# Inverse spectra in DRAM kept by partition, all of step 4 stored, and a new order of the first loads

## The chip, the cores and the metric

One core of a Trainium2 chip runs the kernel. The metric is device time in microseconds: the median of 3 runs of the kernel before is 442.58 us (442.55 to 443.0). One further execution was profiled: it took 444.42 us, of which its span, from the first to the last instruction that the profiler saw, is 442.6 us. All times below that stand beside a place in the schedule are counted from the start of that span. Lines are those of the kernel before.

## What is computed

The kernel is the forward and backward pass of two branches on the same input, S = 2048 tokens, D = 512, F = 1376. All ten results are returned: the output and nine gradients.

```python
xn = layernorm(q)
# branch A: a long convolution over tokens and channels, by FFT
k_shift = sum_t pad(k)[t:t+S] * shift_k[:, 3-t]
kv = k_shift * v
y  = irfft2(rfft2(pad(kv)) * rfft2(pad(ssm_k)))[:S] + kv * ssm_D
A  = xn * y
# branch B: a bilinear GLU
h  = (xn @ w_gate) * (xn @ w_up)
B  = h @ w_down
out = q + A + B            # and jax.vjp of this for grad_out
```

## The kernel before

**Layout.** The 2048 tokens stand as 128 partitions by R = 16 rows. F is cut into 6 steps j of 256 columns (step 1 has 96), in the order of the list `SF`. Everything lives in one SBUF tile `big` (and one PSUM tile `PP`), so the profile names nearly every tile `big`, and nearly every instruction carries line 172, the recording helper. Tiles are told apart by the DRAM tensor at the other end of a transfer, by shape and by time.

**Stages.** (1) Head: `xload`, `gtload`, `gload` and the weights arrive; `ln` (L369) computes the row statistics and normalises x in place; `tr_rows` (L384) transposes two rows on TensorE; `mlp_rows` (L391) does the matmuls of a row pair with the weights of step j. (2) `glu_gen` goes through the 6 steps. The three products of a row (h, and two factors for the gradients) go into a ring of 24 slots in SBUF, `ring(j, r)` (L273), and `hd_store` (L408) writes them to the DRAM tensor HD, four rows at a time: one store of 768 KB. Steps 0, 2 and 3 and the narrow step 1 are stored whole; of step 4 (NST - 2) only the rows below `KEEP` = 8; step 5 is not stored. `dw_all(j)` computes the weight gradients of a step, 96 matmuls. (3) Branch A's transform in three DRAM passes: `a_gen` (first DFT, about 25 to 125 us, into AX), `s_gen` (about 130 to 275 us): it loads AX, does the middle DFT `s_B`, the products `s_pw`, the inverse middle DFT `s_Bi` with the table ET, and stores the inverse spectra to the DRAM tensor CX. (4) `turn_gen` (L559) transposes the products that were not stored on TensorE, 128 by 128 each, 8 to a PSUM tile, with one ACT copy for each 8: 8 rows of step 4 and 16 rows of step 5, 6 blocks a row, 144 transposes and 18 copies. (5) F, from about 290 us: 8 chunks n of two rows. `c_load(n)` (L613) brings 1536 KB of CX into `f["C"]`, `last_dft` (L652) does the last DFT with the table W2, and `c_y`, `c_dkv`, `c_o5`, `c_dsk`, `dk_pair` make branch A's outputs. `y_o` and `y_x` (L719, L732) do 33 matmuls of 128x512 a row with the transposed products.

**How HD comes back.** `hd_load(m)` (L581) is a transposing DMA of one row m: 640 columns for an even row and 512 for an odd one while m < KEEP, 512 and 384 from there on (the missing 128 columns are step 4's, turned on TensorE). Even rows have two buffers `hdE` (each also holds a part that the odd row beside it reads), odd rows have one buffer, `hdO`. So the load for row 2n + 3 can start only when row 2n + 1 has been multiplied.

**How CX lies.** CX has 128 by 32 entries of 3 KB (three signals of 512 columns), each padded to 3,136 bytes. The first index is a frequency q = 4g + k, the second a row index r of 32. `s_Bi` leaves a tile whose partition is (k, r); it is stored through the view `(g k) r e -> (k r) g e`: neighbouring partitions write neighbouring entries. A chunk's load reads, for each of 128 q, two pairs of entries, 100,352 bytes apart from one q to the next.

**What sets the order.** The program is first recorded as operations with a due time (`at(t)`), and `emit` then issues them in the order that the string `PLAN` holds (it also holds the PSUM place of each tile). All DMAs, loads, stores and transposing loads alike, are issued by SyncE (SP), in that order, so one that waits holds back all behind it. The first loads have due times from -10 on, in the order of L341 to L355. 32 matmuls on a tile of ones (8 of 512 columns, 24 of 128; L319 to L323) come ahead of any data.

Of the kernel before, what the change touches and what calls it, by code (L numbers as in the profile page):

```python
# [11 lines left out]
F32 = mybir.dt.float32  # L12
ALU = mybir.AluOpType
# [16 lines left out]
KEEP = 8  # L30
EPS = 1e-5
PLAN = "c-lpG0~98^?{<;~UE8*8+qP}nwr$(CZQHi(y?1y2@4NSRzHg?JO!M?fnw*|aCpI7e!~uf1kOtyGd`JKe5(0yOLLxBm5CTF%C<qN<AS{G~@DKqaLL`U`Q6MTrgXoYIVn9rY1*IV|WP|Kb268|W$O-wO9^`_gkOy)@eaH(1pfV(bd{7X|LKP?kRUtW)hr&<}ia<3e3dNv06o=-J0xCcWr~x&h7Sx7H&<RpPNoWDRpboTz&d>mQLtUr{sh}0~fkx088bTZB3*Dd{^n=DQ4oX26Xae0~0i=eu&=vYaQy2>EVIcH?W-tsoz`rm6IzmsF0pnpIM8cUc9MZ!em;fVT5sZL|Fc=oYBp3yoVF;v!$uJty!5CNtOCU4Mf+?^Xrovd51505xEQ94R4d%iYSOL>vD`bIruoAYxeAo+XAOmcNeXtI8z*^V^J7GV3hV}3fzQArc02$#RY=k|q0gl2~I0VPx8)SlGa2QU)5jX+g;WC_pi|`xH!Fjj>Kj0EvfYT5U<6{C$h-aV+cEv<^4IaQ%_z8(|6LiCe&>eeVXzYoP;2*dSk0A-3qojBPlHnit1<CO&5T?MCm<m%PVj4_~PvADB!(P}ML*P^BgLj}WJ_o>I_zXtiC+LU6u|JN)QP>zAHo?)@6dA|j7z~BYP;nDB#}?QUL*hefg@&!M4TizC*bdvHU<V9~v#}#~!Z{cYJx<5YI1|I;0GxpXaTX53!8i|ZLIfOwm9R3-#amDiBVuGMgoUvP-i4yL8dqQxya&bbK19XhSOQC8DU61tu?&{Qa#$XtV+E{&Rk0dY#8ns*W8fOBj&X1$*1(#00&8JyT#K==4mO~57#m-}D_D<p@g>y5xY&^D;|6Siuc0B<p+>k7H{%-^iU+YS)uVm*7T&`+d<XSu5`KUQI36csdYp(EFe6UIop=B<;S}73hwuw!#>F@dvtU*{j7u;Z?!oMs1CL-%%!Ru#H|D{km>2WmLfnh_@fdEwMOXj_(tO;8CvhoW!K-);uj388iMMbB-Nrk(AMfHlypIp?AwI&#_ynKgR(yuf@ddub<M;|+;~RX7@9;f-z}oZ?KjCNmf?x3)e#am96aT^O_%Hs#-}nau3xJ3mF$pOdc?v-xDHMgKFcg-;QFw|#3os%@qVu>6n@~Txh!-$2?Z8Xej0R8?DoLfNDV3%&G>FPlIch=8=`s$c<dlL^QYvamsVNPmr6H7#(o+V?NSP=zWudH;jmpzdsz4Q~5@n|xv>bC%E;@z7C^zMys5FoAQa;L01*jkuqLEaXiqLc_O2w!+Ri-LbmHJaPDnY}kI@O?P6rEyFO^QjeC^p5RMsynEQap-J3Fr(?p@fu(5>paNN@uY#b);l8o?6j4>_n}pElr|{)P~yA1nNoCr~|d58PuI7Q!naFqi81epf0qEu2C&oN3&=(eWl*ChQ`ut8bj-;E3KueG@9nn2AWUZXd~^Xy)=&I(gE5{eP|z@r=_%q4$>CtOBZMbEvId?j5g6B+D<F!B5kFgw3#l^zw{67qy==D&d@K~K}YEdEvB=yhz`>++C>ZLJ3XSSbexXR54uAy=>#pI-*l2<x>zo@yHAfPj*IK!xqB4f-K7NX8zpp!Tw?cxlDMQUnfpT_+*1nUPSFDj>DYyJ&jJfT+;eL0PE&H{+zU$KLb;Sq-E|7>I=Jxe26c3uTxWNay0}}^)eUsv+<UrBgIqWFkv>p&*TeO6y<BhiiTb#{uAdv~`n%8ciiWwtE|q&juPL=l<I=ixF1>q88C*t}$z^s!To(6^vbt<;xXbQxxSXz@tM78T2CkuN<Z`>lu8C{vnz`n#g=^_RTDjKl54Uk`U0GMowR7bixI8YeLzmCxcOzT@H_4fc;wC%q3c5%xs*B(vyD2W3i|AOUy6A4S6H$rb#=0@iWSkr6LWq}XZoC`iP^P;I&Iw6espu-Xcv9I_aaG+6SIt#-A*F_^>1w&!u8y1FX1Tg9tW0$CTxgl;R=7|y-z{+~-E6nag_osnj$7`+Nf?PQtK3|-*hP>+E};~5MO;KF>LN)omq3cU$dX7(xFk~2t#(^oR7orgTvFNQO1WfGLQ1>na@{R-#bu2v<D$q7mt1bTMedfn?bf<G?ykG%V#s~>z(tdXE~ccG0WOw2a%ttUd*WitQx`{`xik`*GfNmwC(m72&LZJBgM{Z}?zlVQ(o1%Uz$qk$oOD?wm7H>?T{b!6a>`kkQqH+da^B^VGLl;^xQtR(^2kMZ$>o*H?usiXS6z9@ClUFYi^LmTMS0;0N&#8tDo7#8FaNkA@~_+IN=ji_?|!*b(ou@ZZ}-O)l}-Y@$sv~(;?1sx)RV}(#nqB19F?Q7<GNB)n1w5eas#O%`(1r$B9&#YYb?eGTr;UE`<&;dQe8rDNNy+xT_Xv_&83cPch#hYymW_LH>oW<+$+~oUc2t{#<h~Su8q8N?_CdRE1l)A`{24td->=-xg+kg`{KIDSJzs;xpvZ1zPk?6TV~4-my72}FUiKaxxWmTpDsENkQf}3vvVwt!*O|_jFxyjLUM3y9wa$=jO=tnBoD{u!IFUcNM26JyWA*A#EE&N^phmK+a={>JXVr(UrE8kWUlOSDS5oilcO#ZkCUM?QRYiJ&cK;@f=rc3vRE>5Dqbq7ISZHIX);C9a4}BLOC&ANkWyTdC(A5ZAk(EZFO*}FmGkjYDZ_<$k<66*T!0JnMp-EZxj3(qqFjzwOA)TbTcrY*<;q;1*GNU)B-MDG)ZnVTR<=nkuEI6BIxmyj{EZv%7Fi*6xj!$L0lY&t$Ur_Wb+{q#l0m#)Hp^f>AwzhNwBnO8l()+;9?m1UH6M^uvQJv@PB|loWVeju(=v+B%4j|!E&08S;k`1J&&vlH$NQxox8Z{_o-fNesn6~Bu(an6d__9)9qGiKxeH&Fu6#jmOE<nG-MI%pke=L&@5@E$&G)1a_vO2CO&&=<KEgNTp&aE2e2kCt6FI@x<s?6rTk=Jo$tnIOr}?Iw;j{cy&hb}i#4qHdyp+cLouA8j{v>bY0$=1y{7NqKXKBXo<h6X4E8LW?adZADF*TOHm5JPzf5>mS&XX8)GMi4}2mD7+RUh(Hp2kk6b11#XA+-sU{v-E!2LF-}I+Jg)*D(5TU|X8Sp*6PN=Gh!hS?6$AjiYlpg3jalyny5C4GypIbRqxXoBW6)X?%^WcX%^L(=Ggy6X;e>s8KYAZsW&%UnA;v-oc4=Cr8y?yqov%6HcUiIlAuSB)Xq7Xfi#(2l)^$;-tEm(`zbS!iRY&XVPVSM^o!^&ZsLmo37+loJO~6R$a}>HHYrdyP93s@Ke60Yk3`~)DN6RGixqQq3b!FZs3i)S3mMyPOC3?6X(-?nnz#pRnDm|d8fYSPh3EEX<mKDx%CZy=KNY%|K<1mjEm|Q{>tUFh?du1Tuh&H1udw>b+^9didsnvX$h^YRkWj4)oQv&OKK-At(~=tcGYfLO1o<h?Ww)AtoGJE+E>eHKkcu-d4TTMfjUSB>jAB<HMFMI(%M=_>*^34s`Yf3F43jBOo!_TU9Ky1rLNMax?0!hT3x5>b%Soy-?~XR>uo)#TXeEc(L*{_r|ES4hiB+aou#vNj?UG2I$sy)LS3XIb(AjF(K<%Q>Np**^>u<y)CSs6C+Sgrpj-8rHqwXsSsUwNZKAKWsXozW+FV=cBW<Zi^qIEO*7`=<=yPqWAN0C@)mPe1Z|Gyas_*ose$w`u&(7*cy{2z9k#*27dQQ)4V!Ng9^`c(T@0!G3DBC4XYA;pnhi+3fZ(+>rr-rbw7Slr6WesWJ?27)Q-}IM;xBQmOPU`?WuK#KQJEIXSmc=o$6B^NCTR|&kajm!&vUpa);@e66qa`hYozjFB$-tsoa*J%vQdnq<Vks?}MYmLz+G1E5%WByzt);UJR^D=0ddp}Ptd!-nik90lS!t_ebu61@w)$4t8dw!8Y)!1HHMKHU!&+K3%VI^WmDRPfR@7SCK+9wGtf95Bwl>JBTO%86Bdn%1wjox_Mp}0}XrrvQHM7yy&YD|$>tLO1qD`{N*3mj!PwQe+tgDT&7B<xu*gP9=)2x>*wdvNw#@aILYs+nx&9GIr$X44zTVq3Qt*x+iHq(aLdYf&F?U2o}4c5=*+78=jhi#K>wo7)zF54D6YFq7!?X;`5&92#XyJ5HOt-Z6G*3I5qF1uxSY`A@}?Y7cB+I+ifdF_+kvvT&?mKYlQFZRv8+IRb5y=|90wEOnccH206VK42KowWY;+RoZ3``7l_X}e%i{5d;gQT-E(=AYUli|!v=41dgG`s4P@`dBRg#>DTpxc<4t_UZftQ~%5M*l&yD&BycUeR%JE2LHz*`HVh-Pw3BECLiCEPwDqs0{_60`OyA^IiJ}l^%pIbKVVsWVxQV4@mYNspWTP>VSP4V#3%RRd{rOP=ke8i4iCP%&*>xjGCr3t>dX2xzML=SYxv^6yszm?_*x!)K406X^(lNEpVzna^?U_i*Vp&0d?R1kxAql%e&5cw@r8VQU%+?pp?p*Sk9G7-d^6w4m-L-|bKl1g_6>X&U&?p&-Th=g#ZUD^{50RqH}pgObl<}d^D}%;Khu}?z5E<s*w69>{cxYi_w%#;Hb34+_H%t-zua&4{rx1r!w>R1{Q$qn@A3=$2*2A`@*DjgzsZmEZT)7y*AMi${b;|!AMyMA7C*+X^ke-2zsisE^ZaVR-=FfQ{Tbib&-VxY8b8XP^)37oztEraYkhBj$e;IB{0)EDU-0Yvb-&eL_V@h*f6+hmH~k~O*kAHX{bPT{Kk>KxRlm$X_3QmL|H9w)8~ihW$3OQI{7Zk=zw#6PTmQ~~@E`qAf6O2E_xx-B-oNpm{0aZrpY&!dYHEQau<(EH0j<n|eZg4&vjt9A!V*9r@K*>7q=EL|KntGA0&sw65CAEN2A-h903757N2vYB`zzUkKtKco{Xcu41sH*t9Do8W)nG^qb^=#WG6$i+2lPJ^2Rv)gzXd6Or3B%>LxQe?mjwNBAo_nd2c-t)AIJbSXbC2x6x95`F+l&xzZMQsh&h;eaFYDj!v7;{kQsCpEY{yD1!D)R7f3LWHUG`)Zz2I#!CC!J1(OZvfC?5TVC4Vb3sz4553vrLHv"
# [4 lines left out]
def kernel(  # L37
# [224 lines left out]
    std = rc.tile("std", [128, R], F32)  # L262
# [18 lines left out]
    nc.vector.memset(eps_t[:], EPS)  # L281
    ra = Region(*RA)
# [38 lines left out]
    for i in range(24):  # L321
        now[0] = -40.0 + i
        MM(at0[:, 0:128], lhsT=ones1[:], rhs=ones1[:], start=True, stop=True)  # L323
    now[0] = -10.0

    def xload(r, n):
        ld(xn[:, r:r + n, :], x_d[:, r:r + n, :])
# [15 lines left out]
    xload(0, 2); step()  # L343
    ld(Wl[0][:, 1024:3072], w_d[:, 1024:3072]); step()
    xload(2, 2); step()
    gtload(1, 1); step()
    xload(4, 4); step()
    gtload(2, 2); step()
    ld(SK[:].rearrange("p j d -> p (j d)"), bass.AP(tensor=sk_d.tensor, offset=sk_d.offset, ap=[[0, 128], [1, 4 * D]])); step()
    xload(8, 4); step()  # L350
    gtload(4, 2); step()
    xload(12, 4); step()
    gtload(6, 2); step()
# [15 lines left out]
    def ln(r0, n):  # L369
        for r in range(r0, r0 + n):  # L370
            nc.vector.bn_stats(stats[:, r % 4, :], xn[:, r, :])
            nc.vector.bn_aggr(mv[:, r, :], stats[:, r % 4, :])
        gs = slice(r0, r0 + n)
        nc.scalar.activation(std[:, gs], mv[:, gs, 1], ACTF.Sqrt, bias=eps_t[:, 0:1], scale=1.0)
        nc.vector.reciprocal(rstd[:, gs], std[:, gs])
        if 2 <= r0 <= 8:
            STT(c1[:, r0 + 1:r0 + 2], mv[:, r0 + 1:r0 + 2, 0], -1.0, rstd[:, r0 + 1:r0 + 2], op0=ALU.mult, op1=ALU.mult)
        for r in range(r0, r0 + n):
            if 2 <= r0 <= 8 and r > r0:
                nc.scalar.activation(xn[:, r, :], xn[:, r, :], ACTF.Identity, bias=c1[:, r:r + 1], scale=rstd[:, r:r + 1])  # L380
            else:
                TS(xn[:, r, :], xn[:, r, :], mv[:, r, 0:1], rstd[:, r:r + 1], op0=ALU.subtract, op1=ALU.mult)
# [117 lines left out]
    def s_Bi(i):  # L500
# [13 lines left out]
        for s in range(2):  # L514
            dst = CX.rearrange("(g k) r e -> (k r) g e", k=4)[:, 4 * i + 2 * s:4 * i + 2 * s + 2, :]
            st(dst, sp["C"][s][:].rearrange("p g t d -> p g (t d)"))
# [96 lines left out]
    def c_load(n):  # L613
        r0 = 2 * n
        ld(f["C"].rearrange("q (h r) e -> q h r e", h=2), CX.rearrange("q (h r) e -> q h r e", h=2)[:, :, r0:r0 + 2, :])
# [148 lines left out]
    def glu_gen():  # L764
        for j in range(NST):
            n = 3 if j == 1 else 8
            for p in range(8):
                t = TJ(j) + n / 2 * p
                at(t)
                if j == 0:  # L770
                    if p == 0:
                        ln(0, 2)
                        tr_rows(xn, xnT, 0, VCOPY)
# [130 lines left out]
def _tables():  # L904
# [6 lines left out]
    w2 = 2 * np.pi * np.outer(2 * (q // 2) + 1, np.arange(64)) / 256  # L911
    w2 = np.where((q % 2 == 0)[:, None], np.cos(w2), -np.sin(w2))
# [82 lines left out]
```

## Time and profile before

| What | Before |
|---|---|
| Median of 3 runs | 442.58 us |
| Profiled execution, its span | 444.42 us, 442.6 us |
| TensorE (PE) busy | 423.1 us, 96% |
| VectorE (DVE) busy | 353.2 us, 80% |
| ScalarE (ACT) busy | 266.0 us, 60% |
| DMA moved | 124.12 MB, mean 280 GB/s |
| `CX<-big` stores | 16 of 768 KB, median 5.3 us to landing |
| `big<-CX` loads | 8 of 1536 KB, median 8.3 us to landing |
| `HD<-big` stores | 14 of 768 KB (5.9 us), 4 of 384 KB (4.6 us) |
| `big<-HD` transposing loads | 16, median 8.7 us to landing |

A line of the timeline reads: start, duration (us), engine, line, operation, output<-input with shapes, count, and in brackets the idle time just before with what ended it. "SPq" is SyncE's queue: the duration is the time for which the issuing instruction held it. A DMA share near 1 means that the 16 DMA engines were on average busy throughout; it can exceed 1, because packets overlap in the record.

### The profile page before, as it was taken

What the parts mean: (1) busy time and instruction counts of PE and PEld (TensorE: products, weight loads), DVE (VectorE), ACT (ScalarE), POOL (GpSimd) and SP (SyncE); (2) the same over time, 40 slices, a digit from 0 to 9 for tenths busy, and PEclk for the clock granted to TensorE, in tenths of its full rate; (3) what the DMA queues carried; (4) which work ended last, traced back from release to release, by engine and by line L of the source; (5) the groups of instructions that cost most, each with busy time, mean ns of one, the idle gap of its engine ahead of it and who ended that gap; (6) DMA issues with size and microseconds to landing.
All of it is one profiled execution on the core that took longest, in us unless ns stands there. A gap on an engine that the chain in (4) does not pass through costs nothing.

```text
span 442.6 us, 8134 instructions
## 1 busy us (share of the span) xinstructions
PE 423.1 (96%) x3179; PEld 203.9 (46%) x3179; DVE 353.2 (80%) x690; ACT 266.0 (60%) x366; POOL 3.4 (1%) x9
## 2 busy tenths in 40 slices
PE   5999999999999999999999999999999888999895
PEld 3565546745445543334434345465444333444343
DVE  3889577799934899979999994055797959999897
ACT  3796778488652579999999998386324013321311
POOL 1000000000000000000000000100000000000000
PEclk9699999999999999999999999999999999999999
DMA  8988769999856768957578779999999999999992
GB/s 263 408 290 306 287 237 336 342 361 376 314 213 239 279 198 307 315 187 280 211 271 307 285 279 274 282 327 293 294 256 274 277 284 277 275 284 285 239 314 92
DMA packets 96366, 124.12 MB, mean 280 GB/s; under 512 B 53316, under 2 KB 62153, under 8 KB 96328
## 3 DMA queue, kind: packets, MB, share of 16 engines
q1 hardware_dynamic: 96328, 123.60, 87.7%
q8 instruction: 25, 0.41, 0.4%
q14 instruction: 13, 0.11, 0.1%
HBM read 56.57 MB, written 54.04 MB: 250 GB/s over the span
## 4 chain that ended last, share of the span: by engine, by line
PE 71%; DMA 16%; DVE 7%; ACT 2%; SPq 2%; issue 1%; DVEq 0%; ACTq 0%
PE PP L172 71%; DMA big<-HD 8%; DVE big L172 7%; DMA out_dram<-big 2%; DMA AX<-big 2%; ACT big L172 2%; SPq L172 2%; DMA big<-in_x_dram 2%; DMA big<-CX 2%; DVEq L991 0%; ACTq L172 0%; DVEq L172 0%
## 5 line engine op out<-in xcount | busy, mean ns | idle before, releaser
L172 PE MATMUL PP<-big 128*128 128x512 bf16 (+8 forms) x3179 | 423.1, 347 | 14.6 <-DMA big<-HD 5.3
L172 PEld LDWEIGHTS <-big 128*128 128x128 bf16 (+4 forms) x3179 | 203.9, 98 | 233.3 <-issue 69.7
L172 DVE TENSOR_TENSOR big<-big 128x1024 bf16<-128x1024 bf16 (+5 forms) x465 | 267.7, 631 | 52.8 <-ACT big L172 43.3
L172 ACT CAST big<-PP 128x1024 bf16<-128x1024 f32 (+2 forms) x311 | 224.6, 788 | 92.9 <-PE PP L172 81.4
L172 ACT ACTIVATE big<-big 128x512 bf16<-128x512 f32 (+2 forms) x28 | 18.7, 670 | 72.0 <-DVE big L172 54.5
L172 DVE CAST big<-PP 128x512 bf16<-128x512 f32 (+1 forms) x37 | 32.3, 874 | 13.0 <-PE PP L172 11.4
L172 ACT COPY big<-PP 128x1024 bf16<-128x1024 bf16 x25 | 25.1, 1038 | 6.3 <-PE PP L172 6.3
L172 DVE SCALAR_TENSOR_TENSOR big<-big 128x1 f32<-128x1 f32 (+2 forms) x52 | 25.0, 500 | 0.5
L172 DVE TENSOR_TENSOR big<-big,PP 128x512 bf16<-128x512 bf16 (+1 forms) x17 | 10.9, 652 | 7.1 <-PE PP L172 7.0
L172 DVE BATCH_NORM_STATS2 big<-big 128x6 f32<-128x512 bf16 x16 | 10.7, 678 | 6.9 <-DMA big<-in_x_dram 6.9
L172 DVE SCALAR_TENSOR_TENSOR big<-big,PP 128x512 f32<-128x512 bf16 x16 | 10.9, 684 | 4.1 <-PE PP L172 4.1
L172 DVE TENSOR_SCALAR big<-big 128x1 f32<-128x1 f32 (+1 forms) x28 | 7.0, 261 | 0.2
L172 POOL MEMSET big<- 128x1536 bf16 (+2 forms) x3 | 2.8, 950 | 279.1 <-DMA CX<-big 279.1
L172 ACT ACT_TABLE_LOAD x2 | 2.6, 1283 | 0.8 <-PEq L983 0.7
L172 DVE BATCH_NORM_AGGREGATE big<-big 128x2 f32<-128x6 f32 x16 | 2.6, 174 | 0.1
L172 DVE RECIPROCAL big<-big 128x2 f32<-128x2 f32 x8 | 1.3, 157 | 1.3 <-ACT big L172 1.3
L172 DVE DVE_READ_ACCUMULATOR big<-big,PP 128x1 f32 x16 | 1.3, 83 | 0.0
L172 DVE DVE_READ_ACCUMULATOR big<-big 128x1 f32 x16 | 1.3, 83 | 0.0
L172 DVE MEMSET big<- 128x1 f32 (+1 forms) x2 | 0.2, 112 | 0.8 <-PEq L983 0.8
L172 DVE COPY big<-PP 128x1024 bf16<-128x1024 bf16 x1 | 0.7, 692 | 0.0
masks.py:199 POOL TENSOR_SCALAR_AFFINE_SELECT big<-big 128x128 bf16<-128x128 bf16 x1 | 0.3, 294 | 0.0
masks.py:197 POOL MEMSET big<- 128x128 bf16 x1 | 0.2, 205 | 0.3 <-POOLq L983 0.3
(4 smaller groups left out, 0.4 us busy)
## 6 DMA issues: line engine op xcount, KB each, us to landing
AX<-big SPq DMA_DIRECT2D x16, 768.0 KB, 4.8
big<-AX SPq DMA_DIRECT2D x16, 768.0 KB, 5.0
CX<-big SPq DMA_DIRECT2D x16, 768.0 KB, 5.3
big<-CX SPq DMA_DIRECT2D x8, 1536.0 KB, 8.3
out_dram<-big SPq DMA_DIRECT2D x44, 256.0 KB, 3.3
HD<-big SPq DMA_DIRECT2D x14, 768.0 KB, 5.9
big<-in_v_dram SPq DMA_DIRECT2D x16, 256.0 KB, 4.7
big<-in_w_dram SPq DMA_DIRECT2D x4, 768.0 KB, 8.0
```

The lines of the kernel that those rows point to most:

```text
L172: o.fns.append(lambda: f(*[fix(x) for x in a], **{kk: fix(x) for kk, x in k.items()}))
```

## The change

Five edits and a new order.

1. **CX.** Its first index is now the partition of `s_Bi`'s tile, its second the group g. The store is a plain copy of partition to partition (two entries in each). The columns of ET are permuted so that one chunk's 4 rows times 2 components stand in 8 neighbouring partitions, once for each j. A chunk's load becomes two DMAs of 768 KB, each reading 8 x 32 entries that lie one after the other, into 64 partitions. W2's rows are permuted to match.
2. **KEEP = 16.** All of step 4 is stored to HD; `turn_gen` does step 5 alone; every `hd_load` has the long form.
3. **First loads.** Rows 0 and 1 of x come by one DMA each, row group 1 of goT ahead of the second part of the weights, later ones in smaller pieces, SK after all of x and goT.
4. **Layernorm.** A square root on a constant is issued at the start; `std` goes, the reciprocal works in place; rows 0 and 1 are done one by one instead of together. Nothing else in `ln` differs in what it does for a pair of rows.
5. **Matmuls on ones:** 8 of 128 columns in place of 24.
6. **PLAN** is another string: order and PSUM places of everything may differ.

```diff
-KEEP = 8
+KEEP = 16
...
+    nc.scalar.activation(s1[:, 0:1], eps_t[:], ACTF.Sqrt)
...
-    for i in range(24):
+    for i in range(8):
...
     gtload(0, 1); step()
     ld(Wl[0][:, 0:1024], w_d[:, 0:1024]); step()
-    xload(0, 2); step()
+    xload(0, 1); step()
+    xload(1, 1); step()
+    gtload(1, 1); step()
     ld(Wl[0][:, 1024:3072], w_d[:, 1024:3072]); step()
     xload(2, 2); step()
-    gtload(1, 1); step()
-    xload(4, 4); step()
-    gtload(2, 2); step()
+    gtload(2, 1); step()
+    xload(4, 2); step()
+    gtload(3, 1); step()
+    xload(6, 2); step()
+    gtload(4, 2); step()
+    xload(8, 4); step()
+    gtload(6, 2); step()
+    xload(12, 4); step()
     ld(SK[:].rearrange("p j d -> p (j d)"), ...); step()
-    xload(8, 4); step()
-    gtload(4, 2); step()
-    xload(12, 4); step()
-    gtload(6, 2); step()
...
-        nc.scalar.activation(std[:, gs], mv[:, gs, 1], ACTF.Sqrt, bias=eps_t[:, 0:1], scale=1.0)
-        nc.vector.reciprocal(rstd[:, gs], std[:, gs])
+        nc.scalar.activation(rstd[:, gs], mv[:, gs, 1], ACTF.Sqrt, bias=eps_t[:, 0:1], scale=1.0)
+        nc.vector.reciprocal(rstd[:, gs], rstd[:, gs])
...
         for s in range(2):
-            dst = CX.rearrange("(g k) r e -> (k r) g e", k=4)[:, 4 * i + 2 * s:4 * i + 2 * s + 2, :]
-            st(dst, sp["C"][s][:].rearrange("p g t d -> p g (t d)"))
+            g0 = 4 * i + 2 * s
+            st(CX[:, g0:g0 + 2, :], sp["C"][s][:].rearrange("p g t d -> p g (t d)"))
...
     def c_load(n):
-        r0 = 2 * n
-        ld(f["C"].rearrange("q (h r) e -> q h r e", h=2), CX.rearrange("q (h r) e -> q h r e", h=2)[:, :, r0:r0 + 2, :])
+        for j in range(2):
+            b = 64 * j + 8 * n
+            ld(f["C"][64 * j:64 * j + 64], CX[b:b + 8].rearrange("(r c) g e -> c g r e", c=2))
...
                     if p == 0:
-                        ln(0, 2)
+                        ln(0, 1)
+                        ln(1, 1)
                         tr_rows(xn, xnT, 0, VCOPY)
...
+    et = et.reshape(128, 16, 2, 2, 2, 8, 2).transpose(0, 1, 2, 5, 4, 6, 3)
```

## The prediction

> **What bounds the kernel now.** I read the page's slices first, then the chain that ended last, then the windows and the timeline of the two stretches that the change touches: the head (0 to 40 us) and the passage from the inverse DFT into F (240 us to the end).
>
> ```profile
> span 442.6 us, 8134 instructions
> ...
> PE   5999999999999999999999999999999888999895
> ...
> DVE  3889577799934899979999994055797959999897
> ...
> PEclk9699999999999999999999999999999999999999
> DMA  8988769999856768957578779999999999999992
> ```
>
> A slice is 11 us. TensorE is full from slice 2 to slice 32, so matmul work taken out there, or started earlier ahead of it, should shorten the run; it is short in the first slice and in F, from slice 33 (about 350 us) on. The DMA share lies at 9 from slice 24 to the end: in F the transfers are as full as TensorE. The clock drops in slice 1.
>
> The chain of waits (start, us, what) shows where F's start hangs on transfers and not on TensorE:
>
> ```profile
> 246.34 36.23 PE PP L172 x321
> 282.57 7.34 DMA big<-CX
> ...
> 289.95 5.09 PE PP L172 x40
> 295.04 0.02 issue
> 295.06 1.51 ACT big L172 x2
> ...
> 296.59 6.57 DMA out_dram<-big
> ...
> 303.22 7.88 DMA big<-HD
> ```
>
> But TensorE had other work meanwhile: its idle time at 289.95 is 0.18 us (ended by CX) and at 311.14 is 0.41 us (ended by HD). Over the whole run the waits table gives:
>
> ```profile
> PE PP L172 <- DMA big<-HD: 5.3, 6, 1.5
> ...
> PE PP L172 <- DMA big<-CX: 1.3, 2, 1.1
> ```
>
> **Part 1, the head.** The timeline of the first rows:
>
> ```profile
> 7.11 0.18 DVE L172 BATCH_NORM_AGGREGATE big<-big 128x2 f32<-128x6 f32 x1
> 7.33 1.28 ACT L172 ACT_TABLE_LOAD   x1
> 8.62 0.30 ACT L172 ACTIVATE big<-big 128x2 f32<-128x2 f32 x1
> ...
> 12.70 10.69 PE L172 MATMUL PP<-big 128*128 128x512 bf16 x60 [0.79 <-DVE big L172]
> ```
>
> The table load of 1.28 us stands between the statistics of rows 0 and 1 and their square root. The early square root on a constant moves it to the start, where ACT idles until 6.72: 1.28 us off the path. Row 0 now has 640 KB queued up to and with it instead of 768 KB; at the 295 to 326 GB/s of 3 to 5 us that is 131 KB / 310 = 0.4 us earlier. Row by row, the first scaling overlaps the second row's statistics: row 0 landing at 5.2, statistics to 6.0 (0.69 + 0.18); row 1 landed by 5.6, statistics to 6.9; square root 0.30, reciprocal 0.15 and scaling 0.41 for each row, the second done at about 8.0, against 10.66 before. It costs one more 305 ns square root and one more 157 ns reciprocal, both inside that sum. The transposes and their copy took from 10.66 to 12.64, so the first 512-column matmuls could start near 10.0 instead of 12.70: 2.7 us. Not all of it survives. The x rows behind the first two now have 1792 KB queued up to and with them instead of 1536, that is 262 KB / 350 GB/s = 0.75 us later than the 9.13 us at which DVE began on them, and from 15 to 30 us DVE is busy 13.64 and ACT 13.81 of 15 us: they, not TensorE (14.11), set the pace, and the change leaves their work as it is. What an earlier start surely fills is DVE's idle time of 0.25 + 0.83 us in 15 to 17 us. Upper end: 2.7 us and part of the slow clock: the granted clock is 0.50 from 11 to 17 us with TensorE busy 5.2 us, which at the full clock would be 2.6 us; half of that, 1.3. Lower end: 0.5, half of DVE's idle time. I take **2.0** (0.5 to 4.0), between DVE's 1.1 and the first matmul's 2.7.
>
> [...]
>
> 16 fewer matmuls on ones (24 of them took 1.5 us) cost nothing: the array waited 3.3 us for data behind them. Moving SK behind 1 MB of x and goT costs nothing while branch A starts at 24 us or later; the SP queue issues all first loads in 0.4 to 0.8 us each, with three issues more (1.2 us), spread over ten microseconds in which the DMA engines are full anyway.
>
> **Part 2, KEEP = 16, TensorE.** 48 of the 144 turning transposes go, and 6 of 18 ACT copies at 1038 ns. From the list by shapes between 255 and 275 us:
>
> ```profile
> L172 PE MATMUL PP<-big 128*128 128x128 bf16 x32 | 2.4, 219 | 0.0
> ```
>
> 32 take 2.4 us, 75 ns each, so 48 take 3.6 us, in a stretch (258 to 283 us) where TensorE is busy 25.00 of 25.00 us. The ACT copies (6.2 us) go from where ACT is busy 9.4 and 9.3 of 10 us (250 to 270). Lower end: 0, if the chain of transfers above (CX load, gradient store, first HD loads) doesn't move up with TensorE. Upper end: 4.5, with some waits on ACT. That store starts when the last weight gradient is done, which is TensorE's work, so most should move: I take **2.6**.
>
> Two more 768 KB stores of HD (0.4 us of SP each, 5.9 us to landing) fall between 160 and 240 us, where the DMA share is 0.74: nothing, and their rows are read 100 us later. Were that cover gone they would cost 1.57 MB / 260 GB/s = 6 us.
>
> **Part 3, KEEP = 16, DMA in F.** Eight transposing loads grow by 128 columns x 1,536 bytes = 197 KB each, 1.57 MB together. At F's 250 to 290 GB/s that is 5.4 to 6.3 us of DMA time, and while it is issued the SP queue stands still. SP in F, the loads for rows 7 to 15 that could go only when a row was multiplied:
>
> ```profile
> 350.07 7.89 SPq L172 DMA_TRANSPOSE big<-HD  x2
> 366.86 7.32 SPq L172 DMA_TRANSPOSE big<-HD  x1
> 386.87 8.08 SPq L172 DMA_TRANSPOSE big<-HD  x1
> 403.30 7.51 SPq L172 DMA_TRANSPOSE big<-HD  x1
> ```
>
> Behind a held SP stand the chunk's stores and its v, KS, x, k and CX loads; DVE's next products wait for these. Yet the trace holds its own comparison. The odd rows' loads start at 331.66, 350.07, 366.86, 386.87, 403.30 and 420.68: the chunks between the first three (long loads) took 18.4 and 16.8 us, mean 17.6; those between the last three (short loads) 16.4 and 17.4, and the mixed one 20.0, mean of these three 17.9. Long loads show no longer chunks. Ends: a loss of 6.3 (all DMA time on the path) and a gain of 0.5; I take a **loss of 0.5**, near the comparison.
>
> **Part 4, CX.** Bytes are the same. A load becomes two issues, and an issue of `big<-CX` in F held SP for 0.63 us: 8 x 0.63 = 5 us more of SP, against 5 to 14 us in each chunk in which SP waits for TensorE; hidden, and 5 us if SP had no such waits. Reading one block after another may run faster: around the first load (282 to 290 us) the core moved 318 GB/s, in its best 2 us 421. Were all loads to gain that, 1.57 MB x 8 would take 30 instead of 39.6 us of DMA time. Nothing in the trace shows whether order in DRAM matters, so the gain is bounded by TensorE's waits for CX and HD, 1.3 + 5.3 us. The other way, the stores now scatter: 16 stores, DMA share 0.74, hidden but for the last, ahead of the first load; a store as slow as the old load (8.3 us for twice the bytes) would cost nothing, one twice as slow as now 5.3 us. I take a **gain of 0.9** (loss of 5.3 to gain of 6.6), part of the CX wait.
>
> [...]
>
> **Sum.** 442.6 - 2.0 - 2.6 + 0.5 - 0.9 = 437.6 us of span. Around the span lie 1.8 us (444.42 - 442.6). The runs' median of 442.58 is 1.84 below the profiled execution, so the same difference of 5.0 gives 437.6 for the median: **437.6 us**, its own range 434 to 441.5. A difference of 0.2%, 0.9 us, is about what runs of this kernel can tell from none. PLAN is not readable from the diff: how its new order shifts waits is part of every range here.
>
> **The rivals.** *The HD loads decide (slower).* `hdO` is single, so rows 9 to 15's loads start only when the row two before is done; TensorE already waits for HD in that half (1.22, 0.44, 0.48 us). From the point where a load lands later than the row ahead of it ends, each of the 8 pays its 197 KB in full, 0.75 us at 262 GB/s, 6.0 together, and the second CX issue goes behind it. With the head at its lower 0.5 and the transposes at 1.0: 442.6 - 1.5 + 6.0 = **447.1**. For it: DMA share 1.05 to 1.10 in every chunk of F. Against: the chunks' comparison. *Gains don't arrive (same).* F starts on its transfers whatever TensorE has done: parts 2 and 4 at 0, part 3 at 0.5, the head at 0.5: **442.6**. For it: the chain at 282 to 311 us. Against: 0.18 and 0.41 us of wait there. *Everything arrives (much faster).* Faster CX reads take DMA time out of F and the waits on HD and CX go: 4.0 + 3.6 + 4.0: **431**. For it: 421 GB/s in the best window. Against: DVE is busy 15.8 us of a chunk of 17.5 on average, the next floor. *The load isn't faster at all* (the edit doesn't do what it says): 437.6 + 0.9 = 438.5, within the forecast.
>
> **How the numbers follow.** Forecast 0.53, much faster (below 434) 0.16, same 0.09, slower 0.22. Faster by over 0.2% is 0.53 + 0.16 = 0.69. The range of 8 in 10 reaches to 432, about half of the much faster case, and to 445, with the lighter half of the slower one.
>
> **What would show it.** Head: a table load before 3 us, first 512-column matmuls on data near 10 us, PE's x count by 30 us larger. Transposes: 128x128 matmuls down by 64, 16 of ones and 48, ACT copies of 128x1024 bf16 by 6. F: chunk lengths between odd HD loads at or below 17.6; CX landing below 8.3 us for both halves together. The prediction is wrong if F's waits on HD grow beyond 5 us, if the first CX load waits for slow stores, or if the new order opens waits in the full stretch from 40 to 280 us.

## The result, and the profile after

| | Before | After |
|---|---|---|
| Median of 4 runs | 442.56 us (441.65 to 443.0) | 477.35 us (477.1 to 483.5) |
| Profiled execution, its span | 444.42 us, 442.6 us | 477.14 us, 475.4 us |

The kernel became slower: 1.0822 times the time of before (95% interval 1.0734 to 1.0911), 34.8 us. The prediction was 437.6 us.

The page of the kernel after, its span and slices (a slice is now 11.9 us):

```profile
span 475.4 us, 7966 instructions
...
PE   6899999899999999999999996997969797858886
...
PEclk8999999999999999999999998897979989989999
DMA  7998889998945686785867898899999999999962
GB/s 251 407 404 304 306 322 350 368 358 304 365 157 187 244 278 215 279 327 200 311 235 251 282 283 228 207 246 269 244 255 228 265 236 272 263 220 284 242 171 89
```

Up to slice 24 (counted from 1, to 285 us) TensorE is about as full as it was, and the first CX load is issued at 283.57 us against 282.57. From slice 25 on, which is F, TensorE is no longer full and its clock has holes, though the DMA share still reads 8 or 9. From the first CX load's issue to the end of the span pass 191.8 us, 160.0 before: nearly all of the loss lies in F. The last lines of the same page, the DMA issues (count, size, median us to landing):

```profile
big<-CX SPq DMA_DIRECT2D x16, 768.0 KB, 7.3
```

A half of a chunk's load lands after 7.3 us; the whole load took 8.3 us before. SyncE's queue and TensorE around the first load show what that means, in the timeline of the kernel after (start, duration, and in brackets the idle time before with its cause):

```profile
283.57 1.33 SPq L172 DMA_DIRECT2D big<-CX  x2
...
310.70 4.12 SPq L172 DMA_TRANSPOSE big<-HD  x1
```

```profile
295.21 12.77 PE L172 MATMUL PP<-big 128*64 128x512 bf16 x103 [4.30 <-DMA big<-CX]
...
349.73 25.51 PE L172 MATMUL PP<-big 128*64 128x512 bf16 x118 [3.78 <-DMA big<-CX]
379.59 12.30 PE L172 MATMUL PP<-big 128*128 128x512 bf16 x57 [3.16 <-DMA big<-HD]
424.69 1.46 PE L172 MATMUL PP<-big 128*128 128x512 bf16 x3 [5.28 <-DMA big<-HD]
```

From the load's issue to TensorE's first matmul on it pass 11.6 us (7.4 before, 282.57 to 289.95), and TensorE now idles 4.30 us where it idled 0.18. The next HD load, behind it in the queue, goes out at 310.70 instead of 303.22. The waits table, lines of TensorE (us in total, times, longest):

```profile
PE PP L172 <- DMA big<-HD: 15.3, 6, 5.3
...
PE PP L172 <- DMA big<-CX: 8.4, 3, 4.3
```

They were 5.3 and 1.3 us: 17.1 us more. The stretch from 290 to 430 us, in both kernels' windows (window, length, busy us and count of PE, PEld, DVE, ACT, POOL, granted clock, DMA share, GB/s), after and then before:

```profile
290.00:430.00 140.00, 114.07 (x582) 49.45 (x591) 92.93 (x186) 38.27 (x44) 0.00 (x0) 0.90 1.05 243
```

```profile
290.00:430.00 140.00, 132.62 (x750) 59.38 (x749) 118.00 (x241) 45.66 (x51) 0.00 (x0) 1.00 1.05 279
```

The DMA engines' share is 1.05 in both, but it carries 243 GB/s instead of 279. The engines are busy and move less: that is the result in one number. The clock column shows a second loss, 0.90 granted against 1.00; it stands behind the idle gaps. In the list of groups by shape, the last DFT's matmuls on the CX data, after and before:

```profile
L172 PE MATMUL PP<-big 128*64 128x512 bf16 x96 | 16.1, 477 | 9.5 <-DMA big<-CX 8.4 <-DVE big L172 1.1
```

```profile
L172 PE MATMUL PP<-big 128*64 128x512 bf16 x96 | 11.9, 382 | 1.3 <-DMA big<-CX 1.3
```

The same 96 matmuls take 477 ns each instead of 382. Two of the long idle gaps stand right before such matmuls: the 12 behind the 4.30 us gap take 634 ns each, the 12 behind the 3.78 us gap 630, and from 296 to 300 us the granted clock is 0.50, from 352 to 356 us 0.54. Over 2 us windows from 282 us on, TensorE's busy time times the share of the clock it wasn't granted sums to 11.3 us after, and to 0.0 before.

### The profile page after: what moved, and what is told of

The parts are those of the page before. It is cut to its first block, busy times and chain, and to the rows that moved or that the text cites. A ratio compares the mean times of both kernels' runs of the same rounds, so it can differ in the third digit from the quotient of the medians.

```text
span 475.4 us, 7966 instructions
## 1 busy us (share of the span) xinstructions
PE 427.1 (90%) x3061; PEld 203.0 (43%) x3115; DVE 353.4 (74%) x691; ACT 259.4 (55%) x361; POOL 3.4 (1%) x9
## 5 line engine op out<-in xcount | busy, mean ns | idle before, releaser
L172 PE MATMUL PP<-big 128*128 128x512 bf16 (+9 forms) x3061 | 427.1, 354 | 44.7 <-DMA big<-HD 15.3
L172 DVE TENSOR_TENSOR big<-big 128x1024 bf16<-128x1024 bf16 (+3 forms) x465 | 268.6, 630 | 95.5 <-ACT big L172 49.0
L172 PEld LDWEIGHTS <-big 128*128 128x128 bf16 (+5 forms) x3115 | 203.0, 99 | 268.3 <-issue 89.3
L172 ACT CAST big<-PP 128x512 bf16<-128x512 f32 (+2 forms) x311 | 223.7, 785 | 99.8 <-PE PP L172 89.0
L172 ACT ACTIVATE big<-big 128x512 bf16<-128x512 f32 (+3 forms) x30 | 19.2, 641 | 109.7 <-DVE big L172 109.7
L172 ACT COPY big<-PP 128x1024 bf16<-128x1024 bf16 x19 | 18.5, 1030 | 2.9 <-PE PP L172 2.9
L172 DVE RECIPROCAL big<-big 128x2 f32<-128x2 f32 (+1 forms) x9 | 1.4, 155 | 0.3 <-ACT big L172 0.2
```

The costliest lines, as they stand in the source:

```text
L172: o.fns.append(lambda: f(*[fix(x) for x in a], **{kk: fix(x) for kk, x in k.items()}))
```

## The experiments

Every variant but one runs its operations in the order of the kernel before, carried over to its edit, so that the effect of an edit is not mixed with the new PLAN; the exception, the fourth, has the order of the kernel after.

**1. Transfers alone.** Only stores into CX-like tensors and loads of them, four chunks back to back, in the old and the new layout.

```diff
+ld(w, v)                                            # OW, old layout, one load
+for j in range(2): ld(w[64*j:64*j+64], v[64*j:64*j+64])   # OH, old, by partition halves
+for j in range(2): ld(w[:, j], v[:, j])             # OR, old, by entries, 128 partitions each
+for j in range(2): ld(c[64*j:64*j+64], NH[b:b+8]...)      # NH, new layout, as the change
+... second half issued by ScalarE                   # NA
```

> Only transfers: none of the computation is done, the outputs are filled with zeros. The spectra buffer is stored 3 times through the old view and 2 times by partition, then loaded in five forms, each form 4 chunks of 1536 KB back to back, twice: OW old layout in one load; OH old layout in two loads of 64 partitions; OR old layout in two loads of 128 partitions and half the entries; NH new layout in two loads of 64 partitions on one queue; NA the same with the second half issued by ScalarE's queue. Theory 'halves' (a load into 64 partitions is slow, whatever it reads): OW and OR take 15 to 17 us for 4 chunks (370 to 420 GB/s), OH and NH 25 to 30 us (210 to 250 GB/s), NA near OW. Theory 'layout' (reading one block after another is slow): OW, OH and OR alike, NH and NA slow. Theory 'neither' (the loads are not the cause): all five alike within 10%.

Windows over each group of four loads, in this order: OH, OR, NH, NA, OW (its second round; window, length, DVE, POOL, clock, DMA share, GB/s):

```profile
187.80:219.00 31.20, 0.00 (x0) 0.00 (x0) 1.00 0.99 210
219.60:237.50 17.90, 0.00 (x0) 0.00 (x0) 1.00 0.97 364
238.20:269.50 31.30, 0.00 (x0) 0.00 (x0) 1.00 0.98 209
269.90:292.50 22.60, 0.00 (x0) 0.00 (x0) 1.00 0.96 290
293.20:311.00 17.80, 0.00 (x0) 0.00 (x0) 1.00 0.96 361
```

Two halves of 64 partitions moved at 209 to 210 GB/s, in the old layout as in the new. One load, or two that each fill all 128 partitions, moved at 361 to 364. The layout in DRAM, which the change is about, made no difference to loads in halves (210 and 209 GB/s); the new layout in one load of 128 partitions was not tried, so whether it matters at 361 GB/s is open. The cut into partition halves took 1.7 times the DMA time (361 to 364 against 209 to 210 GB/s). With the second half on ScalarE's queue the rate is 290; the expectation had put it near that of the whole load. The DMA share is 0.96 to 0.99 in all of them. Stores went at 393 to 396 GB/s into either layout.

**2 and 3. The CX edit alone, and the cut alone.** Experiment 3 keeps the old layout, its stores and its tables, and cuts only the load.

```diff
 # 2: L515, L613 and the tables as in the change
 # 3: old layout
-ld(f["C"]..., CX...[:, :, r0:r0 + 2, :])
+for j in range(2):
+    qs = slice(64 * j, 64 * j + 64)
+    ld(f["C"][qs]..., CX...[qs, :, r0:r0 + 2, :])
```

> The kernel before with the new CX layout and its two loads alone, everything else and the order as before. If the CX loads cost the time (halves or layout): 460 to 470 us, about 3 us more for each of 8 chunks. If KEEP or the new order cost it: 441 to 445 us.

> The kernel before with its old CX layout, but each chunk's load cut into partitions 0 to 63 and 64 to 127. Theory 'halves': as slow as the CX edit alone, 460 to 470 us. Theory 'layout': 442 to 446 us (eight more issues of 0.6 us on SP, mostly hidden).

Measured: 465.42 us, ratio 1.0526 (1.0452 to 1.0599), and 465.19 us, ratio 1.0517 (1.045 to 1.0584), against 442.29 for the kernel before beside them. The two can't be told apart: within these intervals the cut into halves accounts for all 23 us. Their windows from 290 to 430 us, and TensorE's waits, experiment 2 and then experiment 3:

```profile
290.00:430.00 140.00, 120.36 (x646) 52.80 (x659) 100.12 (x201) 40.35 (x45) 0.00 (x0) 0.94 1.05 243
...
PE PP L172 <- DMA big<-CX: 11.9, 5, 3.3
PE PP L172 <- DMA big<-HD: 10.0, 5, 2.9
```

```profile
290.00:430.00 140.00, 120.30 (x646) 53.02 (x659) 100.19 (x203) 40.36 (x45) 0.00 (x0) 0.94 1.05 242
...
PE PP L172 <- DMA big<-CX: 12.6, 5, 3.3
PE PP L172 <- DMA big<-HD: 10.3, 5, 4.6
```

They carry 243 and 242 GB/s, as in the kernel after. In experiment 2 TensorE waits 11.9 us for CX and 10.0 for HD, 15.3 more than before, and loses 7.4 us to the clock by the same sum over windows: 22.7 us. The spans of the two profiles differ by 20.5 us, the medians by 23.1.

**4. The change without its CX edit**, in the order of the kernel after.

```diff
 # against the kernel after: L515, L613 and the tables as before
-for j in range(2): ld(f["C"][64 * j:64 * j + 64], ...)
+ld(f["C"].rearrange("q (h r) e -> q h r e", h=2), ...)
```

> The changed kernel with its old CX layout and one load of 128 partitions a chunk put back, in the changed kernel's order. If the halves cost 23 us here as on the old order: 454 us, and the other edits together with the new order cost about 12 us against before. If they cost more beside the long HD loads (an interaction): 446 us, near KEEP = 16 alone.

Measured: 454.45 us, ratio 1.0254 (1.0179 to 1.0329): 22.9 us below the kernel after. The CX edit costs the same from either side. But 11.7 us of loss stay, in which it has no part.

**5. Two loads that each fill 128 partitions**, half the entries each, in the old layout.

```diff
-ld(f["C"]..., CX...[:, :, r0:r0 + 2, :])
+for j in range(2):
+    ld(f["C"][:, 2 * j:2 * j + 2, :], CX[:, 16 * j + r0:16 * j + r0 + 2, :])
```

> The kernel before with each chunk's load cut in two in the other way: 128 partitions each, half of the entries. If the partition halves are the cause: 442 to 444 us. If two loads in place of one are the cause: 465 us.

Measured over 10 runs: 441.69 us, ratio 0.9976 (0.9943 to 1.0009). As many issues as in the change, and no loss:

```profile
290.00:430.00 140.00, 133.47 (x751) 59.42 (x748) 120.56 (x248) 45.08 (x51) 0.00 (x0) 1.00 1.03 282
```

282 GB/s and a full clock. The second issue by itself cost nothing here; whether it gains anything can't be told.

**6. The second half from ScalarE's queue**, so that both halves can be in flight together.

```diff
-ld(f["C"][64 * j:64 * j + 64], ...)
+(nc.scalar.dma_start if j else ld)(f["C"][64 * j:64 * j + 64], ...)
```

> The kernel before with the new CX layout as in e2, but the second half of each load issued on ScalarE's queue, so that both halves can be in flight side by side. From the rates measured alone (210 GB/s in halves, 285 with two queues, 363 whole): a chunk's load costs 5.5 us instead of 7.5 (4.3 whole), so 8 x 1.2 = 10 us over before: 452 us. If the split as such cost the time (more issues, more completions): 465 us as in e2.

Transfers alone had shown 290 GB/s for this (NA, experiment 1). Measured: 475.89, 470.36, 459.7 and 468.22 us. The runs lie too far apart for an interval, and the one profile is of the slowest of them. All lie above the expected 452, and why is open.

**7. Which partitions make a load slow.** Transfers alone: loads of 768 KB into partitions 0 to 63, 32 to 95, 64 to 127, and of 1536 KB into all; then transposing loads of 640, 512 and 384 rows, as F has them.

```diff
+for u, p in ((P0, 0), (P32, 32), (P64, 64)):
+    for n in range(8): ld(c[n % 4][p:p + 64], u[p:p + 64, 4 * n:4 * n + 4, :])
+for n in range(4): ld(c[n], SRC[:, 4 * n:4 * n + 4, :])
+for b in (640, 512, 384): ...dma_start_transpose(out=place[...][:, :, 0:b], in_=HT[0:b, :])
```

> Only transfers: none of the computation is done, the outputs are filled with zeros or left. Loads of 768 KB into 64 partitions, 8 back to back: into partitions 0 to 63 (P0), 32 to 95 (P32) and 64 to 127 (P64), beside loads of 1536 KB into all 128 (SRC); then transposing loads of 640, 512 and 384 rows, four of each. If which partitions are written together sets the rate: P0 and P64 near 210 GB/s, P32 well above, up to 363. If the number of partitions sets it: all three near 210. Transposing loads: a rate for each size; if they are slower by the byte than plain loads, 197 KB more cost more than the 0.75 us that I took.

Windows over each group, in the order 0, 32, 64, all; then 640, 512, 384 (columns as in experiment 1):

```profile
243.00:275.00 32.00, 0.00 (x0) 0.00 (x0) 1.00 0.99 204
276.50:293.50 17.00, 0.00 (x0) 0.00 (x0) 1.00 0.97 371
295.00:327.00 32.00, 0.00 (x0) 0.00 (x0) 1.00 0.99 204
328.00:345.00 17.00, 0.00 (x0) 0.00 (x0) 1.00 0.98 371
347.00:363.00 16.00, 0.00 (x0) 0.00 (x0) 1.00 1.08 224
365.50:379.00 13.50, 0.00 (x0) 0.00 (x0) 1.00 1.00 212
381.50:392.00 10.50, 0.00 (x0) 0.00 (x0) 1.00 0.96 190
```

64 partitions weren't slow as such: 32 to 95 took 371 GB/s, the rate of all 128. The lower 64 alone and the upper 64 alone took 204, and the change's two loads are just these. The transposing loads moved at 190 to 224 GB/s with next to nothing beside them.

**8. KEEP = 16 alone.**

```diff
-KEEP = 8
+KEEP = 16
```

> The kernel before with KEEP = 16 alone: step 4 is stored whole, 48 transposes and 6 copies go, 8 transposing loads grow by 197 KB; the order is otherwise as before. My prediction's step: 440.5 us (2.6 gained, 0.5 lost). Theory 'KEEP decides' (the long HD loads are on the path): 448 us or more.

Measured over 10 runs: 446.1 us, ratio 1.0082 (1.0042 to 1.0122): 3.8 us slower, between the two expectations, where the prediction's two KEEP terms together gave 2.1 faster.

**9. The head alone**: first loads, layernorm row by row, 8 matmuls on ones, early square root. **10. Head and KEEP = 16 together**, in the order of before.

```diff
 # 9: items 3, 4 and 5 of the change        # 10: and KEEP
-ln(0, 2)
+ln(0, 1)
+ln(1, 1)
```

> The kernel before with the head edits alone (new first loads, early table load, rows 0 and 1 one by one, 16 fewer matmuls on ones), the reciprocal and scaling of rows 0 and 1 placed ahead of row 2's statistics on VectorE, all else in the order of before. My prediction's step: 2.0 us faster, 440.7 us (438.7 to 442.2). If VectorE and ScalarE set the head's pace whatever the first rows do: 442.2 to 443.2 us. In the changed kernel the row 2 statistics stand ahead of row 1's reciprocal and wait 3.1 us for x; here the first 512-column matmuls should start near 10 us, there they started at 13.05.

> Head edits and KEEP = 16 together, in the order of before: all of the change but the CX edit and the new PLAN. If the parts add: e9 plus 3.8 us, about 444.5 us, and the new order (454.45 us in e5, which has the same edits) costs some 10 us. If the edits themselves interact and the order is innocent: 452 us or more.

Measured: 444.15 us over 12 runs, ratio 1.0033 (1.0001 to 1.0065), and 448.08 us, ratio 1.0131 (1.0092 to 1.017). The head gains nothing (in experiment 9 the first 512-column matmuls on data start at 13.14 us, where near 10 was expected), and KEEP adds 3.9 us to it, the 3.8 of experiment 8 again.

The kernel of experiment 10 and that of experiment 4 do the same work and differ in PLAN alone: 454.45 - 448.08 = 6.4 us (by their ratios to the kernel before, 1.2%, 5.4 us). TensorE's waits for HD, experiment 4 and then experiment 10:

```profile
PE PP L172 <- DMA big<-HD: 11.6, 5, 5.3
```

```profile
PE PP L172 <- DMA big<-HD: 5.2, 3, 2.5
```

They differ by 6.4 us too, while the spans of these two profiles differ by 7.4: in the new order TensorE comes to more of its matmuls before their HD loads have landed. The intervals of the two ratios only just lie apart (from 1.0179, up to 1.017), and PLAN also holds the PSUM places, so order and places aren't separated.

**11 and 12. Why the head gains nothing.** The kernel after has DVE in this order (its timeline):

```profile
10.29 0.69 DVE L172 BATCH_NORM_STATS2 big<-big 128x6 f32<-128x512 bf16 x1 [3.11 <-DMA big<-in_x_dram]
10.90 0.15 DVE L172 RECIPROCAL big<-big 128x1 f32<-128x1 f32 x1
...
12.34 0.66 DVE L172 COPY big<-PP 128x1024 bf16<-128x1024 bf16 x1
```

The square root of row 1 was done at 7.5 us, yet DVE stands 3.11 us: in its order the statistics of row 2, whose x arrives at 10.3 us, come ahead of row 1's reciprocal and of the copy that the first 512-column matmuls need. Experiment 9 put the reciprocals and scalings of rows 0 and 1 first, experiment 11 the copy too, and experiment 12 also took the old order of the loads behind the first two rows.

```diff
 # 11: DVE's order in the head
 BATCH_NORM rows 0, 1; RECIPROCAL and scaling of rows 0, 1
-BATCH_NORM rows 2, 3; COPY (transposes of rows 0, 1)
+COPY (transposes of rows 0, 1); BATCH_NORM rows 2, 3
 # 12: and L346 to L355 as before
```

> As e9, but the transposes of rows 0 and 1 and the copy of their result also stand ahead of row 2's statistics, so that nothing of the first two rows waits for the next x rows. If that place in VectorE's order is what held the first rows back in e9 (copy at 12.41 us): copy near 9.8, first 512-column matmuls near 10.5 us, and 440 to 442 us overall. If the later rows set the pace (x of rows 2 and 3 landing at 10.5 instead of 9.1 us): first matmuls early, but the time stays at 443 to 445 us.

> As e11 in the first rows, but with the loads behind x rows 0 and 1 in the order of before (second part of the weights, x rows 2 and 3, then goT), so that rows 2 and 3 land near 9.1 us again. If the new order of loads is what costs the head its gain: 440.5 to 442 us, ahead of e11 and of before. If neither matters: within 0.2% of before, 441.5 to 443.3 us.

Measured: 443.01 us, ratio 1.0015 (0.9978 to 1.0052), and 443.64 us, ratio 1.0022 (0.9987 to 1.0058): as before. In experiment 12 row 2's x came at 10.02 us, not near 9.1, so the old place in time was not reached. The timeline of experiment 11 shows why an early copy brings so little:

```profile
8.99 0.69 DVE L172 COPY big<-PP 128x1024 bf16<-128x1024 bf16 x1 [0.49 <-PE PP L172]
...
11.70 1.29 DVE L172 BATCH_NORM_STATS2 big<-big 128x6 f32<-128x512 bf16 x2 [0.45 <-DMA big<-in_x_dram]
...
14.42 0.40 PE L172 MATMUL PP<-big 128*128 128x128 bf16 x4 [2.78 <-DVE big L172]
```

The copy is done 3.3 us before that of the kernel after. Then TensorE stands 2.78 us until rows 2 and 3 are through: their x arrived at 10.34 and 11.70. The gap was moved by one pair of rows, not removed.

**The sum, and F chunk by chunk.** Cut into halves 22.9, KEEP 3.8, head 1.8, order 6.4: 34.9 us by medians, and 34.8 were measured. These are steps from kernel to kernel, so most of that agreement is built in; what checks it is that the cut and KEEP were each measured twice, with 22.9 and 23.1 us, 3.8 and 3.9. The head's 1.8 is barely clear of no change (its interval begins at 1.0001). The profiles say where. "F begins" is the issue of the third HD load; a chunk is a fifth of the time between the issues of the sixth and the sixteenth HD load:

| Kernel | F begins, us | us a chunk |
|---|---|---|
| before | 303.22 | 17.80 |
| after | 310.70 | 21.23 |
| 2: CX edit alone | 307.81 | 20.31 |
| 3: cut alone | 306.49 | 20.46 |
| 4: after without the CX edit | 302.44 | 19.05 |
| 5: two loads of 128 partitions | 302.46 | 17.18 |
| 8: KEEP alone | 300.63 | 18.19 |
| 9: head alone | 302.93 | 17.68 |
| 10: head and KEEP | 303.51 | 18.41 |

## Why the prediction was wrong

**Part 4, CX, is the step that failed**: "A load becomes two issues [...] hidden", a gain of 0.9 within a loss of 5.3 to a gain of 6.6. It costed the second issue (no loss in experiment 5, ratio 0.9976) and the order in DRAM (without effect on loads in halves, experiments 1 to 3), and took the rate of a load for a property of its bytes. In these runs it went by the partitions that the load writes: 1.57 MB at 364 GB/s is 4.3 us, at 209 it is 7.5, so 3.2 us a chunk and 26 us for eight chunks. The runs lost 22.9 of them. The part had no cover, because F's DMA share was already 1.05; I had read that share myself, and weighed against it only SyncE's time.

The cut alone cost 22.9 us (experiment 3), and not by its second issue. In experiment 7 the number of partitions was the same three times and the rate was not: 204 GB/s into 0 to 63, 204 into 64 to 127, 371 into 32 to 95. What sets the third apart from the other two is not shown. The prediction had no rate of a load into 64 partitions to reckon with; experiment 1 gives one.

**What a late load makes late.** The prediction named a sign in HD's waits (wrong above 5 us, though its own table had 5.3) and the rival in which HD decides, 447.1 us. HD's waits did grow, by 10.0 us, but mostly not through the 197 KB that the rival charged: KEEP alone left TensorE's wait for HD at 6.5 us, the cut alone took it from 5.3 to 10.3. In the kernel after, the larger part is there without the cut: in the new PLAN's order the wait is 11.6 us with the old CX load (experiment 4), and the cut adds 3.7. The HD load after a slow CX load goes out later (310.70 us instead of 303.22); how much of that is SyncE's queue, how much TensorE's lateness and how much the DMA engines wasn't separated. Then the clock: in the kernel after every gap of 3.2 to 5.3 us in TensorE's work has a granted clock of 0.50 behind it for the next microseconds. Shorter gaps go either way: 2.53 us in experiment 10 has 0.51 behind it, 2.87 us in experiment 2 has 1.00. From what length on the clock falls, and why, is not shown. The prediction reckoned with this clock in the head alone.

**Parts 2 and 3, KEEP.** The work went as predicted: 64 fewer 128x128 matmuls with the 16 on ones, ACT copies of 128x1024 down from 25 to 19. In experiment 8's profile F begins 2.6 us earlier, the size of the predicted gain, but that gain isn't shown: with the same KEEP, experiment 10 begins F at 303.51, experiment 9 without it at 302.93. A chunk takes longer in both: 0.39 us more than before in experiment 8, 3.1 us over eight, and in experiment 10 0.74 more than in experiment 9, 5.9 us over eight. The step that failed is the loss of 0.5 read from the chunks' comparison, long ones against short ones. It was also sorted wrongly: between 350.07 and 366.86 us the loads of rows 7 and 8 go out, one long and one short, and between 366.86 and 386.87 those of rows 9 and 10, both short. So one long chunk of 18.4 us stands against three short ones of 17.9 on average, and the long one is the longer. Long loads stood in the first half of F and short ones in the second, so the comparison mixed the loads with all else that differs there. By the rate of transposing loads alone the bytes cost more than the upper end of 6.3: 1.57 MB at 212 GB/s (experiment 7) is 7.4 us. Experiment 8's profile belongs to the fastest of its ten runs, 3.2 us below their median, so how the median's 3.8 us divide is not shown.

**Part 1, the head.** Table load, square root and row-by-row statistics came out as worked out: the kernel after has its second row's statistics done at 7.2 us, and the table load at the start. The gain of 2.0 did not. Two things stood in the way: DVE's order, which put waiting work ahead of ready work, and, with that mended (experiment 11), the arrival of the next rows, which the prediction had named as what may eat the gain and left 2.0 standing all the same. The intervals of experiments 11 and 12 leave room for a gain of about 1 us and for a loss of 2.6.

**The new order** was put into "every range" as unreadable. Experiments 4 and 10 put it at about 6 us, mostly in waits for HD. It was left without a term of its own. One reading of the page was off without effect: TensorE is short of full from the 32nd slice, 343 us, not from about 350.

## What to carry to other kernels

Price a DMA by the partitions it writes before you price its bytes or its order in DRAM: a load cut at partition 64 moved at 0.57 times the rate (209 against 364 GB/s), and a cut along the free axis (the elements within a partition) cost nothing (364 GB/s, and 0.9976 times the time of before in the kernel). Where the DMA share is already 1, count added transfer time as paid until a run shows otherwise: here 22.9 of 26 us were, in waits for the load itself, in waits for other loads, and in a lower clock behind the gaps (7.4 us in experiment 2). A comparison of early with late iterations is no experiment on what differs between them.

## What the runs showed of the hardware

- The DMA share did not tell the rate of transfers alone: 0.99 at 204 GB/s and 0.98 at 371 (experiment 7).
- Two loads into the two halves, issued from two queues, moved at 280 to 290 GB/s together, against 209 in turn on one queue, and 361 for one load into all partitions (experiment 1). Whether it helps in the kernel is unsettled (experiment 6).
- Transposing loads moved at 224, 212 and 190 GB/s for 640, 512 and 384 rows (experiment 7): of these three, the shorter, the slower per byte.
- The padded layout in DRAM, one block or rows 100,352 bytes apart, made no difference to loads in partition halves (210 and 209 GB/s) or to stores (393 to 396; experiment 1).
